# A fused chunk-select attention and ELU MLP on one core: the first batch prepared by four heads, and a step of the ELU moved to another engine

## The chip, the cores and the metric

The kernel runs on one core of one Trainium2 chip. The metric is device time in microseconds, the median of three runs. A core has five engines that work at the same time, each through its own list of instructions in order: PE (TensorE, matrix products), DVE (VectorE), ACT (ScalarE), POOL (GpSimd) and SP (SyncE, which here only issues DMAs).

## The reference

Four batches of eight heads, 768 positions, head dimension 64. For each head the keys are cut into 24 chunks of 32. A query's bound for a chunk is the sum over the 64 dimensions of the larger of q times the chunk's minimum and q times its maximum; the six causal chunks with the largest bounds are kept, and softmax attention runs over the kept, causal keys. The result, 3072 rows of 512, goes through an MLP with ELU in between.

```python
k_min, k_max = np.min(k_chunks, axis=3), np.max(k_chunks, axis=3)
ub = np.sum(np.maximum(q[..., None, :] * k_min, q[..., None, :] * k_max), axis=-1)   # shapes shortened
ub = np.where(causal, ub, -1e9)
top_chunks = np.argsort(ub, axis=-1)[..., -6:]
scores = np.where(sel & (pos[:, None] >= pos[None, :]), scale * q @ k.T, -1e9)
attn = softmax(scores) @ v
h = x @ w_in                                    # x: 3072 x 512, w_in: 512 x 2048
g = np.where(h > 0.0, h, np.exp(np.minimum(h, 0.0)) - 1.0)
out = g @ w_out                                 # 2048 x 512
```

The larger of the two products is computed as q * min + relu(q) * (max - min): one product of the turned queries with the chunk minima, one of their positive parts with the differences.

## The kernel before, in words

Heads go in pairs `u` (16 of them; four to a batch), and two pairs make a quad `g`. Each pair's 768 queries go in two halves `hf` of 384. Scores are computed transposed, keys on partitions and queries along the row, so that the exponentials (ACT, L675) can be used as weights of the products with V (`psO`, L707) without a turn. The selection is added to the scores by the product itself: the score product has 88 rows, 64 of the head dimension and 24 of a one-hot pattern `econ` in `lhs` against a 0/1 row per chunk in `rhs`, times -40000. The output of a pair is normalised (`on`, L720 and L723), turned by PE (`psT`, L732) and copied into `xT` (L735). When all four pairs of a batch have their `xT` for a half, the MLP's first products for it can start.

**The MLP** (`mlp`). For each half of a batch 16 blocks `fc` of 128 hidden units: four products into a bank `psH` (L757), exp on ACT into `e` (L767), and then one of three ways to finish the ELU. In blocks listed in `BOTH`, ACT makes relu in place (L772) and DVE makes min(e - 1, relu) (L775). In the last batch (`FAST`) DVE makes min(e, 1) - 1 and a maximum with h. In all others DVE makes t = max(e - 1, h) (L796) and then min(max(h, 0), t) (L801). The results `gT` go through the second products (`psM`, L814), ACT copies the sums out (L822) and SP stores them. The MLP of a batch runs beside the attention of the next.

**The first batch** (`first_prep`). Nothing can be hidden there. K and Q come in 256-byte rows, 128 positions on the partitions, each half of a pair in a DMA per head (L464; Q of the first two pairs from ACT's queue). PE turns them with an identity (L483, 48 products in float32); ACT copies K into `lhs` (L488) and Q into `qt` (L506), and makes the positive part `qa` (L510); DVE takes minima and maxima per chunk from PSUM (L493) and their difference (L500); POOL casts Q into `rhs` (L526) and V into `vext` (L517). The later batches (`pair_prep`) load in 128-byte pieces, turn on DVE (L403, L421), reduce there (L407) and cast on POOL.

**The selection** (`quad_sel`), for a quad and half: 16 products on tiles of 64 rows and 32 columns (L556), a turn of 32x32 blocks by DVE (L573), the eight largest per query and block (L585), a comparison with the sixth (L590), the turn back into `selt` (L596), and POOL copies of it into `rhs` (L607). The first batch's causal mask is one more product per diagonal block, an identity with `trineg` (L654); later ones are masked by POOL after the exponential (L694).

**The order** is made ahead of time by `Plan`: every operation has an engine, a duration, a priority, what it reads and writes and which buffers it takes; `order` simulates the engines with these durations and always takes what can start first, by priority among those ready. The order on each engine is then fixed in the program. Buffers are limited by `caps`; eight PSUM banks are shared as two double banks `S2` (scores) and four single ones (`ps`, with limits for `psH`, `psO`, `psT`, `psM` and `psMT`). `WHEN` names the operations that must be done before POOL asks for each piece of the MLP's weights.

## Time and profile before

| | |
|---|---|
| median of three runs | 284.86 us (284.71 to 284.96) |
| profiled execution | 283.3 us from the first to the last instruction, 1.56 us under the median |
| PE busy | 263.8 us, 93% |
| DVE busy | 207.3 us, 73% |
| ACT busy | 198.4 us, 70% |
| POOL busy | 125.2 us, 44% |
| granted TensorE clock | 0.976 on average |
| read from HBM, written | 27.26 MB, 6.29 MB |

The profile is one execution, recorded by the hardware. A line such as L757 is a line of the kernel before. Engines overlap, so shares do not add up. "Busy" of PE counts each product from its start to its modelled end, and products are pipelined: the time that a product really costs is the distance from its start to the next start. The same holds, less strongly, for DVE.

### The profile page before, as it was taken

To read this page: it belongs to the slowest core of one execution; us is meant where nothing else is said; L and a number is where in the kernel's file an instruction comes from. 1 tells how busy PE (TensorE), PEld (TensorE's weight loads), DVE (VectorE), ACT (ScalarE), POOL (GpSimd) and SP (SyncE) were. 2 spreads that over 40 slices of the span, in tenths; PEclk is the share of its full clock that TensorE was granted. 3 is DMA by queue.
4 is the path that set the end of the run, shared out by engine and by line. 5 is a ranking of instruction groups with operands and counts; after the bars stand their busy time and mean duration, and the time that the engine had idled before them with its cause. 6 is when DMAs were issued, how large, how long until landed. Compare 5 with 4: busy or idle time off the path is not lost.

```text
span 283.3 us, 7007 instructions
## 1 busy us (share of the span) xinstructions
PE 263.8 (93%) x2584; PEld 160.2 (57%) x2584; DVE 207.3 (73%) x563; ACT 198.4 (70%) x373; POOL 125.2 (44%) x235
## 2 busy tenths in 40 slices
PE   2887599999989999889999999999999999999994
PEld 2676357665546656465655566656565656555541
DVE  8827676798999998899989467967685424767610
ACT  4969379876498569999969967885856764545311
POOL 6547842046399689789558361611132201000000
PEclk9959779999999999999999999999999999999999
DMA  9878999988769899999984010001101101000111
GB/s 169 185 172 176 209 203 198 184 143 158 166 131 170 132 138 195 176 158 138 145 157 94 37 39 2 37 2 39 38 2 38 39 37 39 37 0 37 39 74 74
DMA packets 120993, 29.81 MB, mean 105 GB/s; under 512 B 113792, under 2 KB 117888, under 8 KB 120960
## 3 DMA queue, kind: packets, MB, share of 16 engines
q1 hardware_dynamic: 115136, 24.78, 46.4%
q0 software_dynamic: 4224, 4.19, 9.4%
q10 hardware_dynamic: 1600, 0.39, 0.7%
q8 instruction: 20, 0.33, 0.5%
q14 instruction: 13, 0.11, 0.1%
HBM read 27.26 MB, written 6.29 MB: 118 GB/s over the span
## 4 chain that ended last, share of the span: by engine, by line
PE 70%; ACT 10%; DVE 8%; DMA 5%; issue 3%; POOL 2%; SPq 1%; DVEq 0%; POOLq 0%; ACTq 0%
PE psM L814 18%; PE psH L757 16%; PE psS L648 9%; PE psS L757 7%; PE psMT L814 7%; PE psO L707 6%; ACT pt L675 5%; DMA stage<-in_k_dram 3%; PE psS L556 3%; DMA gT<-in_k_dram 1%; ACT e L767 1%; DVE gT L775 1%; DVE thr L585 1%; PE psT L732 1%; ACT lhs L488 1%
## 5 line engine op out<-in xcount | busy, mean ns | idle before, releaser
L675 ACT ACTIVATE pt<-psS 128x768 bf16<-128x768 f32 (+1 forms) x120 | 90.4, 798 | 6.5 <-PE psS L648 3.8
L757 PE MATMUL psH<-xT,w_in_sb 128*128 128x384 bf16 x384 | 75.9, 330 | 0.0
L814 PE MATMUL psM<-w_out_sb,gT 128*128 128x512 bf16 x288 | 72.2, 379 | 0.4 <-ACT xT L735 0.3
L757 PEld LDWEIGHTS <-w_in_sb 128*128 128x128 bf16 x512 | 48.2, 98 | 34.9 <-issue 2.6
L767 ACT ACTIVATE e<-psH 128x384 f32<-128x384 f32 x96 | 47.7, 518 | 25.2 <-PE psH L757 22.8
L648 PE MATMUL psS<-rhs,lhs 88*128 88x384 bf16 (+4 forms) x304 | 55.1, 292 | 4.2 <-ACT pt L675 1.9
L814 PEld LDWEIGHTS <-gT 128*128 128x128 bf16 x384 | 35.7, 97 | 35.0 <-issue 0.7
L694 POOL TENSOR_SCALAR_AFFINE_SELECT pt<-pt 128x256 bf16<-128x256 bf16 (+1 forms) x48 | 25.1, 527 | 45.5 <-ACT pt L675 42.5
L796 DVE SCALAR_TENSOR_TENSOR t<-e,psH 128x384 bf16<-128x384 f32 x56 | 30.1, 544 | 16.7 <-ACT e L767 16.3
L648 PEld LDWEIGHTS <-lhs 88*128 88x128 bf16 x304 | 29.1, 101 | 17.4 <-issue 5.4
L607 POOL COPY rhs<-selt 24x192 bf16<-24x192 bf16 (+1 forms) x64 | 27.0, 422 | 25.3 <-DVE selt L596 21.4
L526 POOL CAST rhs<-qt 64x768 bf16<-64x768 f32 (+1 forms) x40 | 28.3, 707 | 15.5 <-ACT qt L506 7.7
L707 PEld LDWEIGHTS <-pt 128*128 128x128 bf16 x672 | 28.0, 98 | 11.3 <-issue 3.2
L707 PE MATMUL psO<-vext,pt 128*128 128x65 bf16 x672 | 31.8, 195 | 1.8 <-DVE gT L801 0.8
L801 DVE SCALAR_TENSOR_TENSOR gT<-psH,t 128x384 bf16<-128x384 f32 x56 | 30.4, 547 | 1.1
L775 DVE SCALAR_TENSOR_TENSOR gT<-e,psH 128x384 bf16<-128x384 f32 x40 | 21.3, 536 | 10.9 <-ACT psH L772 8.9
L526 POOL CAST lhs<-kt 64x768 bf16<-64x768 f32 x24 | 19.7, 821 | 19.4 <-DVE kt L403 15.1
L767 ACT ACTIVATE e<-psS 128x768 f32<-128x768 f32 x16 | 13.0, 811 | 18.9 <-PE psS L757 18.9
L757 PE MATMUL psS<-xT,w_in_sb 128*128 128x384 bf16 x128 | 23.2, 326 | 0.0
L814 PE MATMUL psMT<-w_out_sb,gT 128*128 128x512 bf16 x96 | 22.5, 379 | 0.0
L735 ACT ACTIVATE xT<-psT 128x384 bf16<-128x384 bf16 x32 | 16.2, 506 | 8.2 <-PE psT L732 8.2
L772 ACT ACTIVATE psH<-psH 128x384 f32<-128x384 f32 x40 | 20.6, 521 | 0.0
(57 smaller groups left out, 287.4 us busy)
## 6 DMA issues: line engine op xcount, KB each, us to landing
out_dram<-osb SPq DMA_DIRECT2D x24, 256.0 KB, 2.0
stage<-in_k_dram SPq DMA_DIRECT2D x48, 96.0 KB, 4.1
stage<-in_q_dram SPq DMA_DIRECT2D x48, 96.0 KB, 3.6
vd<-in_v_dram SPq DMA_DIRECT2D x24, 192.0 KB, 3.8
w_in_sb<-in_moe_w_in_dram POOLq DMA_DIRECT2D x4, 512.0 KB, 9.4
w_out_sb<-in_moe_w_out_dram POOLq DMA_DIRECT2D x4, 512.0 KB, 9.0
gT<-in_k_dram SPq DMA_DIRECT2D x16, 96.0 KB, 3.0
gT<-in_v_dram SPq DMA_DIRECT2D x16, 96.0 KB, 2.5
```

The lines of the kernel that those rows point to most:

```text
L526: nc.gpsimd.tensor_copy(out=o, in_=i)
L607: eng.tensor_copy(out=dst.rearrange("c h (i two x) -> c h i two x", two=2, x=32)[:, :, :, odd, :], in_=tiles[st][r0:r0 + NCH, c0:c0 + n].r ...
L648: nc.tensor.matmul(p_s[:, hd, pc:pc + w], lhsT=tiles[pt_["kb"]][0:64 + NCH, hd, 128 * kb:128 * kb + 128], rhs=tiles[pt_["qb"]][0:64 + NCH, ...
L675: lambda bs=bs, pt=pt, wtot=wtot, lo=lo, at=at: nc.scalar.activation(out=tiles[pt][:, :, lo:lo + wtot], in_=tiles[bs[0]][:, :, at:at + wto ...
L694: nc.gpsimd.affine_select(out=a, in_=a, compare_op=AOT.is_ge, fill=0.0, base=0, pattern=pat, channel_multiplier=-1)
L707: nc.tensor.matmul(po[:, hd, qi, :], lhsT=tiles[pt][:, hd, off:off + 128], rhs=tiles[pt_["vx"]][:, 6 * hd + kb, :], start=(kb == 0), stop= ...
L757: nc.tensor.matmul(ph, lhsT=w_in_sb[:, kk, f0:f0 + 128], rhs=tiles[XT[4 * b + kk]][:, c0:c0 + HALF], start=(kk == 0), stop=(kk == NKK - 1))
L767: lambda e=e, view=view: nc.scalar.activation(out=tiles[e][:, 0:step], in_=view(), func=AF.Exp),
L775: lambda e=e, view=view, fc=fc, gt=gt: nc.vector.scalar_tensor_tensor(out=tiles[gt][:, fc:fc + step, :], in0=tiles[e][:, 0:step], scalar=1 ...
L796: lambda e=e, t=t, view=view: nc.vector.scalar_tensor_tensor(out=tiles[t][:, 0:step], in0=tiles[e][:, 0:step], scalar=1.0, in1=view(), op0 ...
L801: lambda t=t, view=view, fc=fc, gt=gt: nc.vector.scalar_tensor_tensor(out=tiles[gt][:, fc:fc + step, :], in0=view(), scalar=0.0, in1=tiles ...
L814: nc.tensor.matmul(pm, lhsT=tiles[gt][:, fc, 128 * tt:128 * tt + 128], rhs=w_out_sb[:, fc, :], start=(fc == 0), stop=(fc == NFC - 1))
```

## The change

It touches the first batch, the ELU and the planner.

- **Loads of the first batch** (`first_load`): K and Q come by head, 32 partitions of 6 pieces of 512 bytes (two neighbouring positions), so that four heads of a quad stand on the four groups of 32 partitions; V comes by 128 positions of four heads. The first half's Q is issued from ACT's queue.
- **Turning** (`first_prep`): DVE turns 32x32 blocks of a whole quad at once, 768 elements a partition, with the output regrouped; minima and maxima are taken from that; ACT casts K, POOL casts Q. PE's float32 turns, ACT's copies of K and Q and the difference on DVE go; the difference and its spreading into a block-diagonal `kmd` are on POOL.
- **Bounds** (`first_sel`): four products of 128 rows and 128 columns with `kmd`, for a whole quad and half.
- **Scores** (`first_scores`): each head's scores in two products of 32 rows (dimensions 0 to 31 and 32 to 63) and one of 24 rows that adds the selection, straight from `selt`; the four heads of a quad stand on four row groups. The causal mask is a product of 32 rows and 32 columns per quarter of a diagonal block and head (`below`, `corner`). A piece takes both double banks.
- **`lhs` and `rhs`** get their selection rows and zeros after the first batch, by DMA from `econ` and by POOL.
- **The ELU**: in the first three batches t = min(e, 1) - 1 is made by POOL (`HELP`), and DVE makes max(t, h). `BOTH` has 8, 8 and 4 blocks a half where it had 4, 12 and 4.
- **The planner**: it models the TensorE clock by windows, has a list of corrections to priorities (`RANK`), issues loads by readiness, and the weights wait for other operations. `caps` has two `psO` and two `psT`, and three `km`.

```diff
-BOTH = {0: (1, 5, 9, 13), 1: (0, 1, 2, 3, 4, 5, 8, 9, 10, 11, 12, 13), 2: (1, 5, 9, 13), 3: ()}
-def WHEN(q_in, left, out):
-    return (left(3, 0), out(0, 0), out(1, 0), out(2, 0), left(1, 1), left(1, 1), left(3, 1), left(3, 1))
+BOTH = {0: (1, 3, 5, 7, 9, 11, 13, 15), 1: (1, 3, 5, 7, 9, 11, 13, 15), 2: (1, 5, 9, 13), 3: ()}
+HELP = {0: range(16), 1: range(16), 2: range(16), 3: ()}
+RANK = {
+    80: 17.15, 158: 0.88, 160: 0.85, 178: 0.83, 180: 1.06, 182: 0.96, 184: 0.96, 186: 0.96, 188: 0.97,
...
+        o.prio = prio + RANK.get(o.n, 0.0)
...
+                    rank = o.ready if e == "DMA" and o.raw > -15 else o.prio
...
-            o.end = r + o.dur
+            o.end = r + (self.clocked(r, o.dur, act) if o.eng == "PE" else o.dur)
...
-    caps = {"S2": 2, "ps": 4, "H": 3, "O": 1, "T": 1, "M": 2, "MT": 2,
+    caps = {"S2": 2, "ps": 4, "H": 3, "O": 2, "T": 2, "M": 2, "MT": 2,
...
+    def rows(kb):
+        for hd in range(2):
+            nc.sync.dma_start(out=kb[64:96, hd, :], in_=econ[64:96])
...
+        def load(i, src, h, eng):
+            def f():
+                o0 = 768 * (2 * g + i)
+                eng.dma_start(
+                    out=tiles[sg].rearrange("p a b -> p (a b)")[32 * h:32 * h + 32, o0:o0 + 768].rearrange("c (m x) -> c m x", m=6),
+                    in_=src[4 * g + h, 6 * hf:6 * hf + 6].rearrange("m c x -> c m x"))
...
+        def turn(i, t):
             def f():
+                o0 = 768 * (2 * g + i)
+                nc.vector.transpose(
+                    out=tiles[t].rearrange("p (e m c j) -> p m j e c", e=2, c=32, j=2),
+                    in_=tiles[sg].rearrange("p a b -> p (a b)")[:, o0:o0 + 768].rearrange(
+                        "p (m j e i) -> p m j e i", m=6, j=2, e=2))
...
+        def ub():
+            pu = ps(bu, [P, HALF], F32)
+            for w in range(2):
+                for e in range(2):
+                    src = tiles[qd["qa", hf] if w else qd["qt", hf]].rearrange("p (e t) -> p e t", e=2)
+                    nc.tensor.matmul(pu[:, 0:n], lhsT=tiles[kmd[g]].rearrange("p (w e x) -> p w e x", w=2, e=2)[:, w, e],
+                                     rhs=src[:, e, lo:HALF], start=(w + e == 0), stop=(w + e == 2))
...
+            def sc(segs=segs, bs=bs, chosen=chosen):
+                for (b_, c0, w, pc) in segs:
+                    for e in range(3 if chosen else 2):
+                        for h in range(4):
+                            r = slice(32 * h, 32 * h + (NCH if e == 2 else 32))
+                            lhsT = (econ if e == 2 else tiles[kb][:, e])[r, 128 * b_:128 * b_ + 128]
+                            rhs = tiles[st][r, c0 - SEL0:c0 - SEL0 + w] if e == 2 else tiles[qb][r, e, c0:c0 + w]
+                            nc.tensor.matmul(tiles[bs[h // 2]][:, h % 2, pc:pc + w], lhsT=lhsT, rhs=rhs,
+                                             start=(e == 0), stop=(e == (2 if chosen else 1) and c0 >= 128 * b_ + 128))
+                    x1 = min(4, (c0 + w - 128 * b_) // 32)
+                    for x in range(max(0, (c0 - 128 * b_) // 32), x1):
+                        o0 = pc + 128 * b_ + 32 * x - c0
+                        for h in range(4):
+                            r = slice(32 * h, 32 * h + 32)
+                            nc.tensor.matmul(tiles[bs[h // 2]][:, h % 2, o0:o0 + 32], lhsT=below[r, x], rhs=corner[r],
+                                             start=False, stop=x == x1 - 1)
...
-                fast = FAST[b]
+                help_ = fc in HELP[b]
+                fast = FAST[b] or help_
                 if fast:
-                    add("DVE", 0.32 + 0.00021 * step * HALF, pr,
-                        lambda e=e, t=t: nc.vector.tensor_scalar(
+                    add("POOL" if help_ else "DVE", 0.15 + 0.00090 * step * HALF if help_ else 0.32 + 0.00021 * step * HALF, pr,
+                        lambda e=e, t=t, eng=nc.gpsimd if help_ else nc.vector: eng.tensor_scalar(
                             out=tiles[t][:, 0:step], in0=tiles[e][:, 0:step], scalar1=1.0, scalar2=1.0,
                             op0=AOT.min, op1=AOT.subtract),
```

378 lines of the change are left out of this document (236 added, 142 removed), and 8 rows, old and new, of tables (RANK, caps).

## The prediction

> **What bounds the kernel now.** I read the page's first line, then the busy time of each engine in stretches, cut where the trace changes character, first of all at the first product of the MLP (L757, 34.59 us). Columns: stretch, its length, busy time of PE, PEld, DVE, ACT, POOL with instruction counts, granted TensorE clock, DMA share, GB/s.
>
> ```profile
> span 283.3 us, 7007 instructions
> 0.00:34.59 34.59, 22.88 (x309) 18.58 (x309) 23.43 (x90) 23.06 (x53) 22.44 (x57) 0.86 0.94 181
> 34.59:60.00 25.41, 25.38 (x256) 16.76 (x249) 19.09 (x50) 22.04 (x41) 7.29 (x13) 0.93 1.24 192
> 60.00:100.00 40.00, 39.01 (x426) 22.16 (x425) 38.83 (x114) 27.45 (x51) 28.32 (x49) 1.00 0.85 145
> 100.00:160.00 60.00, 57.38 (x612) 34.88 (x611) 54.31 (x139) 53.61 (x106) 45.86 (x78) 1.00 0.88 145
> 160.00:262.00 102.00, 101.89 (x913) 59.74 (x912) 66.00 (x166) 67.21 (x117) 21.31 (x41) 1.00 0.07 28
> 34.59:38.40 3.81, 3.81 (x21) 1.83 (x14) 3.19 (x18) 1.38 (x3) 2.94 (x5) 0.51 1.42 213
> ```
>
> From 34.59 us on PE is the bound: it is idle 0.03 us up to 60, 1.0 up to 100, 2.6 up to 160 and 0.1 up to 262. Before 34.59 nothing is full; that is the pipe that fills. The last row shows that the first 3.8 us after it run at half clock. So the time is: when the first L757 starts (t1), plus PE's work from there, plus clock lost there, plus PE's few idle moments and the tail. The change can act on each of the first four, and work that PE does ahead of t1 counts only where it delays t1.
>
> What ends the filling is in the timeline (start, length, instruction, releaser in brackets):
>
> ```profile
> 32.69 0.50 PE L732 MATMUL psT<-ident_b,on 128*128 128x128 bf16 x3 [2.95 <-DVE on L723]
> 33.23 0.49 ACT L735 ACTIVATE xT<-psT 128x384 bf16<-128x384 bf16 x1 [2.87 <-PE psT L732]
> 34.59 2.74 PE L757 MATMUL psH<-xT,w_in_sb 128*128 128x384 bf16 x8
> ```
>
> PE waits 2.95 us for DVE's `on` of the fourth pair. From the end of that wait to a possible first product are 32.69, 33.23, 33.72: about 1.1 us.
>
> **Term A, t1.** Removed ahead of t1: 48 PE transposes, ACT's copies of K and Q, and ten DVE copies of `econ`. Added on DVE: eight turns of 128x768. Loads become 36 on SP and 8 on ACT's queue, each 96 KB of 512-byte rows (V 128 KB), where 44 on SP and 4 on ACT stood. First what SP pays for one load, and its landing:
>
> ```profile
> 0.81 3.46 SPq L464 DMA_DIRECT2D gT<-in_k_dram  x6
> 12.08 1.02 SPq L464 DMA_DIRECT2D gT<-in_k_dram  x2
> 13.14 1.02 SPq L464 DMA_DIRECT2D gT<-in_q_dram  x2
> gT<-in_k_dram SPq DMA_DIRECT2D x16, 96.0 KB, 3.0
> ```
>
> Two loads start 1.06 us after the two before them: 0.53 us each, which I keep for the new shapes, since no row here shows that fewer rows are issued faster. The four K of quad 0 start at 0.81 to 2.4 and land at 5.4. DVE's constants take under 4.5 us after 0.9 and are done about then. From there the order of the changed kernel puts on DVE, up to the fourth `on`: nine 128x768 turns, ten reductions, 30 of the MAX8, the bounds' turns, comparisons and turns back, four reciprocals and four `on`. Their cost is start to start in a stretch where DVE runs without a gap:
>
> ```profile
> 145.34 0.58 DVE L573 STREAM_TRANSPOSE ubt<-psS 128x384 f32<-128x384 f32 x1
> 145.98 0.54 DVE L801 SCALAR_TENSOR_TENSOR gT<-psH,t 128x384 bf16<-128x384 f32 x1
> 146.90 1.04 DVE L585 MAX8 thr<-ubt 128x8 f32<-128x14 f32 x12
> 147.87 0.17 DVE L720 RECIPROCAL rc<-psO 128x6 f32<-128x6 f32 x1
> 147.96 0.93 DVE L421 STREAM_TRANSPOSE qt<-stage 128x768 f32<-128x768 f32 x1
> 148.82 0.51 DVE L723 TENSOR_TENSOR on<-psO,rc 128x384 bf16<-128x384 f32 x1
> 149.26 0.53 DVE L796 SCALAR_TENSOR_TENSOR t<-e,psH 128x384 bf16<-128x384 f32 x1
> 153.36 0.95 DVE L407 TENSOR_REDUCE km<-kt 128x24 f32<-128x768 f32 x1
> 154.23 0.54 DVE L775 SCALAR_TENSOR_TENSOR gT<-e,psH 128x384 bf16<-128x384 f32 x1
> 156.09 0.45 DVE L590 TENSOR_TENSOR selv<-ubt,thr 128x288 bf16<-128x288 f32 x1
> 156.45 0.55 DVE L775 SCALAR_TENSOR_TENSOR gT<-e,psH 128x384 bf16<-128x384 f32 x1
> 156.92 0.57 DVE L596 STREAM_TRANSPOSE selt<-selv 128x384 bf16<-128x384 bf16 x1
> 157.41 0.51 DVE L775 SCALAR_TENSOR_TENSOR gT<-e,psH 128x384 bf16<-128x384 f32 x1
> ```
>
> A turn is 0.86, a reduction 0.87, one MAX8 0.97/12 = 0.081, reciprocal and `on` 0.09 + 0.44; the bounds' turn 0.64, the comparison 0.36 and the turn back 0.49 for 384 columns, half of it for 192. So 9 x 0.86 = 7.7; 10 x 0.87 = 8.7; 30 x 0.081 = 2.4; 4 x 0.53 = 2.1; bounds' turns 3 x 0.64 = 1.9 (two full, two halves), comparisons 2 x 0.36 = 0.7, turns back 2 x 0.49 = 1.0: 24.5 us. DVE waits, too. The last K of quad 1's second half is SP's 32nd load: it starts at 0.81 + 31 x 0.53 = 17.2 and lands at 20.2, while DVE, at its own pace, asks for it at about 17.5. The same for quad 0 costs about 0.3 earlier, which shortens the second wait: 2.7 together. `on` ends at 5.4 + 24.5 + 2.7 = 32.6, and with 1.1 + 0.1 for the transposes and the copy t1 = 33.8: **-0.8 us**. The small edits of this stage (memsets and `corner` on POOL, casts of whole quads, the first weights asked for earlier) lie beside this DVE chain. Bounds: no wait for loads gives 31.1; the first weights' 1 MB in the way of the last K and Q, at the 181 GB/s of this stretch, up to 5.5 us: 39.
>
> One link in it grows: the bounds' products. Before, 16 products on 64x32 tiles:
>
> ```profile
> 70.29 0.40 PE L556 MATMUL psS<-qt,km 64*32 64x96 f32 x16
> 70.48 0.37 PE L556 MATMUL psS<-qa,km 64*32 64x96 f32 x16
> 70.78 1.04 PE L814 MATMUL psM<-w_out_sb,gT 128*128 128x512 bf16 x4
> 71.75 0.56 PE L556 MATMUL psS<-qt,km 64*32 64x192 f32 x16
> 72.10 0.53 PE L556 MATMUL psS<-qa,km 64*32 64x192 f32 x16
> 72.56 1.47 PE L757 MATMUL psH<-xT,w_in_sb 128*128 128x384 bf16 x8
> ```
>
> 96 columns take 0.49 us, 192 take 0.81: 0.32 for 96 columns more, and 0.17 fixed. Sixteen products over eight tiles are two deep, so a column costs 0.32/192 = 1.67 ns. Four products of 384 columns, one after another, are then 2.56 us where 0.81 stood. PE has room for that ahead of t1, as long as the clock is full; at half clock two of them add 5 us to PE and about 2.5 to DVE's chain.
>
> **Term B, clock after t1.** Today 3.81 us at 0.51 of the clock lose 1.9 us, after PE's 2.95 us of idling. In the changed order two pieces of quad 0's second-half scores and two pairs' P·V stand ahead of the first L757 in that place, so I take the clock as granted: **-1.9**; the other end is 0.
>
> **Term C, scores left after t1.** Prices: 384 columns, and a short product with its own weights:
>
> ```profile
> 68.41 1.95 PE psH L757 x12
> 239.05 0.70 PE psO L707 x22
> ```
>
> 0.1625 us for 384 columns, 32 ns for a 65-column pair. Left today: four pairs x 2 heads x 1920 columns = 40 x 0.1625 = 6.5, and 24 mask products of 128 columns (a third of 0.1625) = 1.3: 7.8. Left afterwards: 2 quads x 3 products x 1920 columns, four heads at a time on 32-row tiles: 30 x 0.1625 = 4.9, less the two pieces ahead of t1 (1.0); 96 mask products of 32 columns; and the 0.17 fixed per tiled block for 8 pieces, 1.4. A 32-column product lies between 12 ns (16 tiled records start in 0.19 us above) and 32 ns; I take 22, halfway: 2.1. Sum 7.4: **-0.4**. Bounds: at 12 ns and without the fixed part -2.8; with no two tiles at once 4 x 3.9 + 3.1 + 1.4 = 20.1, +12.3. The Trainium skill (TensorE: Matmul & The Clock Gate, section "Wait — 56ns, not 53.3ns?") says that starts of products never come closer than about 25 ns, however short; by it the 96 take 2.4 us and C is -0.1. The 12 ns above stand against it, unless two records are one product.
>
> **Term D, the ELU.** All 56 t move from DVE to POOL, leaving one DVE step per block; two batches' counts of blocks that take ACT's second pass change by +8 and -8.
>
> ```profile
> L796 DVE SCALAR_TENSOR_TENSOR t<-e,psH 128x384 bf16<-128x384 f32 x56 | 30.1, 544 | 16.7 <-ACT e L767 16.3
> L517 POOL CAST vext<-gT 128x384 bf16<-128x384 f32 x8 | 3.9, 507 | 0.3
> L772 ACT ACTIVATE psH<-psH 128x384 f32<-128x384 f32 x40 | 20.6, 521 | 0.0
> 116.54 0.49 PE L648 MATMUL psS<-rhs,lhs 88*128 88x384 bf16 x2 [1.25 <-ACT pt L675]
> 124.89 0.54 PE L707 MATMUL psO<-vext,pt 128*128 128x65 bf16 x12 [0.83 <-DVE gT L801]
> ```
>
> DVE loses 30 us. POOL's t has the size of the cast in the second row; I take its 0.51, and as upper end twice the DVE row, 1.09. Batch 1's 16 t fall largely into 100 to 160: POOL 45.9 + 8.1 = 54 of 60 us, DVE 54.3 - 4.4 = 50, ACT 53.6 - 4.2 = 49: the fullest engine stays near 54. Batch 0's 16 t meet a POOL with room (35.6 of 65.4 us), batch 2's 24 one with more (21.3 of 102). Batch 0's eight extra passes cost ACT 4.2 us where it is busy 22.0 of 25.4; the copies it loses ahead of t1 do not help there, which speaks for some new PE waits. What can be won is PE's idle 3.6 us of 60 to 160, of which the last two rows show the largest: **-1.0**, between -3.6 and, with POOL full, the plus of the first rival. The new fills of `lhs` rows (ten DMAs, 5.3 us of SP) and `rhs` zeros go in once the loads are out; SP's cover is that batch 1's scores are far away: 0, and if that cover is gone 5.3 us at the start of batch 1.
>
> **The sum.** -0.8 - 1.9 - 0.4 - 1.0 = -4.1 on 283.3, so a span of 279.2. The median of the three runs is 284.86, 1.56 over the span of the profiled execution; with the same 1.56, **280.8 us**.
>
> **The rivals.** (1) *POOL becomes the bound of 100 to 160, slower.* For it: POOL is the fullest engine there even at 0.51; against it: the cast row. At 1.09 per t POOL has 45.9 + 17.4 = 63.3 us to do; busy 95% it needs 66.6, so +6.6 in place of -1.0: 288.4. It decides from a t of 0.9 us on: (64 x 0.95 - 45.9)/16, where the stretch grows by what the rest saves. The Trainium skill (GPSIMD Engine Reference, section 4.1, Engine selection) speaks for this: elementwise work belongs on VectorE, GpSimd being about twice as slow; but it limits that to two inputs and calls one input roughly line-rate, and t has one. Chance 0.14. (2) *The turns with regrouped rows cost DVE more.* No row shows them; `on` also writes regrouped and costs 0.44 for 384 columns, against it. At half as much again 8 x 0.43 = 3.4 us: 284.2; at twice 287.7. Chance 0.10. (3) *Late and cold*: the weights delay the last K, and the clock is halved around t1: A +2.5, B 0, so 286.0; milder, 284.5. For it: DMA at 0.94 in this stretch, and PE sparsely used ahead of t1. Chance 0.13. (4) *The tiles do not run side by side*, the change not doing what it says: 280.8 + 12.7 = 293.5 or more. The 64x32 tiles above overlap, against it. Chance 0.06. (5) *DVE's relief shows in full*: t1 32, D -3.6: 276.4. Chance 0.14.
>
> **How the numbers follow.** The forecast has 0.43, with a range of its own of 278 to 283.5 from halves of the bounds of A, C and D. 0.2% (0.57 us) is about what a measurement of this kernel tells from no change. Faster: 0.43 + 0.14 + 0.05 of rivals 2 and 3 in their mildest form = 0.62. Same: 0.08, from 2 and 3 at 284.2 to 285.4. Slower: the other 0.10 of these, and 1 and 4: 0.30. The range 275.5 to 288.5 leaves out the tiles' rival, the dear end of rival 2 and the far ends of 1 and 5, less than 0.2.
>
> **What would show it.** The first up product at 33 to 35 us at full clock (A, B); turns of 128x768 at 0.95 us and DVE without long gaps between 5 and 32 us (A); score pieces of 384 columns, without masks, in about 0.7 us (C); t on POOL near 0.5 us and POOL below 56 us busy between 100 and 160 (D). A t over 0.9 us, turns over 1.2 us, four tiles taking four times 0.16 us, or a first product after 37 us would make it wrong.

## The result: 11% slower, with POOL's step at three times its forecast price

| | before | after |
|---|---|---|
| median | 284.91 us (284.71 to 288.35, 4 runs) | 317.11 us (316.87 to 318.06, 4 runs) |
| profiled execution | span 283.3 us | span 316.3 us, 318.06 us in all |
| first up product (t1) | 34.59 us | 40.66 us |
| span from there | 248.7 us | 275.6 us |

The ratio is 1.109, 95% interval 1.100 to 1.118. Forecast were 280.8 us and a range of 275.5 to 288.5. (Some executions, of the kernel before and of several versions, run at a lower granted clock and take some per cent longer; ratios leave them out.) Both parts of the time went the wrong way: t1 came 6.1 us later than before, and what follows it took 26.9 us more.

The page of the changed kernel: span, busy time by engine, and the chain that ended last by engine and by line.

```profile
span 316.3 us, 7243 instructions
PE 265.6 (84%) x2736; PEld 154.2 (49%) x2736; DVE 186.4 (59%) x485; ACT 194.4 (61%) x349; POOL 200.9 (64%) x283
PE 38%; POOL 31%; DVE 8%; issue 8%; DMA 8%; ACT 4%; SPq 3%; POOLq 0%; DVEq 0%; ACTq 0%
POOL t L939 17%; PE psM L968 10%; PE psS L910 7%; PE psMT L968 7%; PE psH L910 5%; POOL rhs L763 5%; POOL pt L847 4%; DMA gT<-in_q_dram 3%; PE psO L860 3%; POOL rhs L683 2%; DMA gT<-in_k_dram 2%; DVE gT L944 2%; PE psS L806 2%; ACT pt L828 2%; POOL vext L487 1%
```

PE's work is nearly that of before (263.8 us), but PE alone is no longer the bound: `t`, the step that the change moved to POOL, is the largest line of the chain. Stretches cut much as in the prediction (columns as there):

```profile
24.00:40.00 16.00, 10.67 (x152) 6.95 (x150) 12.54 (x47) 7.42 (x13) 7.48 (x12) 0.89 1.14 169
60.00:100.00 40.00, 34.82 (x469) 19.81 (x467) 27.75 (x68) 28.55 (x53) 29.66 (x41) 1.00 0.76 134
100.00:160.00 60.00, 51.12 (x588) 29.66 (x579) 47.60 (x146) 42.06 (x80) 56.52 (x80) 1.00 0.80 133
160.00:260.00 100.00, 89.36 (x831) 52.17 (x829) 47.68 (x135) 68.78 (x126) 78.77 (x94) 1.00 0.10 30
```

Between 60 and 260 us PE is idle 5.2 + 8.9 + 10.6 us, where it had been idle 3.7 in all; POOL is the fullest engine from 100 to 160 (56.5 of 60). The groups of `t` and of the DVE step behind it (count, busy, mean ns, idle time before and its releasers), and the waits:

```profile
L939 POOL TENSOR_SCALAR t<-e 128x384 bf16<-128x384 f32 x56 | 83.3, 1494 | 21.4 <-ACT e L920 18.8 <-issue 1.8
L944 DVE TENSOR_TENSOR gT<-t,psH 128x384 bf16<-128x384 bf16 x56 | 30.9, 552 | 62.1 <-POOL t L939 61.5 <-PE psS L659 0.6
DVE gT L944 <- POOL t L939: 61.5, 48, 3.2
PE psH L910 <- DVE gT L944: 13.1, 18, 1.6
```

One `t` takes 1.49 us where 0.51 was assumed: 83 us of POOL for 56 of them. DVE waits for it 48 times, and PE, whose banks `psH` are freed by that DVE step, 18 times.

The first stretch, on DVE and then on PE (start, length, instruction, wait before it and its releaser):

```profile
6.34 0.97 DVE L548 STREAM_TRANSPOSE kt<-gT 128x768 f32<-128x768 f32 x1
18.56 0.98 DVE L548 STREAM_TRANSPOSE kt<-gT 128x768 f32<-128x768 f32 x1 [3.25 <-DMA gT<-in_q_dram]
26.49 0.98 DVE L548 STREAM_TRANSPOSE kt<-gT 128x768 f32<-128x768 f32 x1 [4.12 <-DMA gT<-in_k_dram]
DVE ubt L619 <- PE psMT L611: 0.9, 1, 0.9
40.66 0.49 PE L910 MATMUL psH<-xT,w_in_sb 128*128 128x384 bf16 x2
41.36 3.40 PE L910 MATMUL psH<-xT,w_in_sb 128*128 128x384 bf16 x10 [0.21 <-ACT xT L888]
```

DVE starts at 6.3, waits 3.3 and 4.1 us for the second half's K, and ten products at 41.36 take 3.40 us: clock is lost here again.

### The profile page after: what moved, and what is told of

Read it like the earlier page. It is cut to its first block, busy times and chain, and to the rows that moved or that the text cites. A ratio compares the mean times of both kernels' runs of the same rounds, so it can differ in the third digit from the quotient of the medians.

```text
span 316.3 us, 7243 instructions
## 1 busy us (share of the span) xinstructions
PE 265.6 (84%) x2736; PEld 154.2 (49%) x2736; DVE 186.4 (59%) x485; ACT 194.4 (61%) x349; POOL 200.9 (64%) x283
## 4 chain that ended last, share of the span: by engine, by line
PE 38%; POOL 31%; DVE 8%; issue 8%; DMA 8%; ACT 4%; SPq 3%; POOLq 0%; DVEq 0%; ACTq 0%
POOL t L939 17%; PE psM L968 10%; PE psS L910 7%; PE psMT L968 7%; PE psH L910 5%; POOL rhs L763 5%; POOL pt L847 4%; DMA gT<-in_q_dram 3%; PE psO L860 3%; POOL rhs L683 2%; DMA gT<-in_k_dram 2%; DVE gT L944 2%; PE psS L806 2%; ACT pt L828 2%; POOL vext L487 1%
## 5 line engine op out<-in xcount | busy, mean ns | idle before, releaser
L828 ACT ACTIVATE pt<-psS 128x768 bf16<-128x768 f32 (+3 forms) x120 | 88.3, 775 | 22.5 <-PE psS L806 12.2
L939 POOL TENSOR_SCALAR t<-e 128x384 bf16<-128x384 f32 x56 | 83.3, 1494 | 21.4 <-ACT e L920 18.8
L944 DVE TENSOR_TENSOR gT<-t,psH 128x384 bf16<-128x384 bf16 x56 | 30.9, 552 | 62.1 <-POOL t L939 61.5
L920 ACT ACTIVATE e<-psH 128x384 f32<-128x384 f32 x96 | 46.4, 499 | 27.4 <-PE psH L910 21.7
L968 PEld LDWEIGHTS <-gT 128*128 128x128 bf16 x384 | 36.1, 98 | 35.9 <-issue 1.1
L806 PE MATMUL psS<-rhs,lhs 88*128 88x384 bf16 (+2 forms) x216 | 38.0, 290 | 2.1 <-DMA out_dram<-osb 1.1
L683 POOL CAST rhs<-qt 64x768 bf16<-64x768 f32 (+1 forms) x28 | 23.2, 828 | 6.3 <-DVE qt L472 4.1
L806 PEld LDWEIGHTS <-lhs 88*128 88x128 bf16 x216 | 19.3, 97 | 12.6 <-issue 2.7
L763 POOL COPY rhs<-selt 24x192 bf16<-24x192 bf16 (+1 forms) x48 | 20.2, 421 | 5.7 <-DVE selt L753 3.5
L976 ACT ACTIVATE osb<-psM 128x512 f32<-128x512 f32 x18 | 10.8, 600 | 16.9 <-PE psM L968 16.9
L659 PE MATMUL psS<-rhs,lhs 32*128 32x384 bf16 (+4 forms) x176 | 9.7, 296 | 13.7 <-ACT lhs L561 9.5
```

Source lines behind the costliest of these rows:

```text
L683: nc.gpsimd.tensor_copy(out=o, in_=i)
L763: nc.gpsimd.tensor_copy(out=dst.rearrange("c h (i two x) -> c h i two x", two=2, x=32)[:, :, :, odd, :], in_=tiles[st][r0:r0 + NCH, c0:c0 ...
L806: nc.tensor.matmul(p_s[:, hd, pc:pc + w], lhsT=tiles[pt_["kb"]][0:64 + NCH, hd, 128 * kb:128 * kb + 128], rhs=tiles[pt_["qb"]][0:64 + NCH, ...
L828: lambda bs=bs, pt=pt, wtot=wtot, lo=lo, at=at: nc.scalar.activation(out=tiles[pt][:, :, lo:lo + wtot], in_=tiles[bs[0]][:, :, at:at + wto ...
L920: lambda e=e, view=view: nc.scalar.activation(out=tiles[e][:, 0:step], in_=view(), func=AF.Exp),
L939: lambda e=e, t=t, eng=nc.gpsimd if help_ else nc.vector: eng.tensor_scalar(out=tiles[t][:, 0:step], in0=tiles[e][:, 0:step], scalar1=1.0, ...
```

## Experiments

### What POOL's step costs

**t back on DVE.** The changed kernel with the ELU of before.

```diff
-BOTH = {0: (1, 3, 5, 7, 9, 11, 13, 15), 1: (1, 3, 5, 7, 9, 11, 13, 15), ...
-HELP = {0: range(16), 1: range(16), 2: range(16), 3: ()}
+BOTH = {0: (1, 5, 9, 13), 1: (0, 1, 2, 3, 4, 5, 8, 9, 10, 11, 12, 13), ...
+HELP = {0: (), 1: (), 2: (), 3: ()}
```

> The changed kernel with the ELU as before: no t on POOL, and the old lists of blocks that take ACT's second pass. Theory P (the price of t on POOL, 1.49 us where 0.51 was taken, carries what is lost after the first up product; the new first batch carries the rest): the first up product stays near 41 us as in the changed kernel, against 34.6 before, and what follows falls back to the 248.7 us of before, so 289 to 292 us. Rival S (the new first batch and its order disturb the later batches as well): over 300. Rival F (the new first batch is no loss by itself, the late t holds it up, too): first up product before 36 us, 280 to 285.

Measured: 289.62 us (287.24 to 290.03), in a later series of runs; span of the profile 285.5, t1 38.89. Going by the two medians, the ELU's part of the change is 27.5 of the 32.2 us. The other parts together still lose, by a late t1: what follows t1 takes 246.6 us, 2.1 less than in the kernel before.

**The ELU alone, in the kernel before.** `BOTH` and `HELP` of the change, POOL's `t` as there.

> The kernel before with the ELU part alone: t of the first three batches on POOL as one instruction of two steps, and the new lists of blocks with ACT's second pass. Theory P: the first up product stays at 34.6 us and the rest grows by about the 26 us by which it grew in the changed kernel, 305 to 314 us, with t at 1.49 us. Rival Q (t is dear only beside the new first batch's traffic): t near 0.5 us and 280 to 287 us.

Measured: 321.81 us (319.53 to 327.06), more than expected: what follows t1 grew by 39.3 us here, and by 26.9 in the changed kernel. Why it is dearer here was not followed. t1 is 33.48, so nothing of it comes from the start:

```profile
L787 POOL TENSOR_SCALAR t<-e 128x384 bf16<-128x384 f32 x56 | 83.4, 1493 | 21.0 <-ACT e L768 19.8
```

The price is the same in another surrounding, 1493 ns: it belongs to the operation, and not to the new first batch's traffic (rival Q).

**One step on POOL in place of two.** POOL makes only min(e, 1); DVE subtracts and takes the maximum in one instruction.

```diff
-  t = (e min 1.0) subtract 1.0      # POOL
-  gT = t max h                      # DVE, two inputs
+  e = e min 1.0                     # POOL, in place
+  gT = (e subtract 1.0) max h       # DVE, scalar_tensor_tensor
```

> The changed kernel with POOL's t cut to one step, min(e, 1) in place in float32; the subtraction goes into DVE's second step, which stays one instruction. If the price hangs on the second step (theory P2), the POOL instruction takes about 0.5 us like a cast of that size, and the time falls to 287 to 293 us, the first up product still near 41. If it hangs on scalar arithmetic on POOL as such (rival P1), it stays at 1.2 to 1.5 us and the time at 310 to 318.

Measured: 303.87 us (302.88 to 304.67), between the two cases. One step takes 1.17 us, far nearer to rival P1 than to the 0.5 of theory P2.

```profile
L939 POOL TENSOR_SCALAR e<-e 128x384 f32<-128x384 f32 x56 | 65.0, 1166 | 23.2 <-ACT e L920 22.4
```

**Prices by themselves.** A kernel with little but POOL instructions, six of each kind (`cp` cast, `min` and `sub` one step, `ms` min and subtract, `am` multiply and add), and min and subtract on DVE (`dv`); the outputs hold zeros.

> A kernel that leaves the computation out and only runs, six times each and one after another, POOL instructions on 128 partitions: a cast of 384 elements from float32 to bf16, one-step minimum and one-step subtraction of the same size, one-step minimum to float32, the two-step minimum and subtraction of 192, 384 and 768 elements, the same to float32 and from bf16, a two-step product and sum; and the two-step form on DVE. Theory P2: casts and one step about 0.5 us, every two-step form 1.4 to 1.5 us at 384, growing with the elements at 3.5 ns each or more. Rival P1: one step as dear as two. Rival M: min alone is dear and product and sum are not. DVE about 0.3 us.

```profile
L87 POOL CAST a_cp<-src 128x384 bf16<-128x384 f32 x6 | 3.2, 540 | 3.6 <-DMA src<-in_moe_w_out_dram 3.6
L91 POOL TENSOR_SCALAR a_sub<-src 128x384 bf16<-128x384 f32 x6 | 7.1, 1178 | 0.0
L95 POOL TENSOR_SCALAR a_ms<-src 128x384 bf16<-128x384 f32 x6 | 9.1, 1509 | 0.0
L99 POOL TENSOR_SCALAR a_ms<-src 128x768 bf16<-128x768 f32 x6 | 16.8, 2798 | 0.0
L105 POOL TENSOR_SCALAR a_am<-src 128x384 bf16<-128x384 f32 x6 | 3.3, 549 | 0.0
L107 DVE TENSOR_SCALAR a_dv<-src 128x384 bf16<-128x384 f32 x6 | 3.5, 586 | 0.2
```

Beside its size (2798 ns for 768 elements) the kind sets the price: one step with a scalar costs 2.2 casts, two steps 2.8, but the pair multiply and add costs one. Min and subtract take 0.59 us on DVE, so the move to POOL made that step 2.6 times as dear. Theories P2 and P1 fell; rival M was right on the pair, but subtract alone is as dear as min alone (1.18 and 1.24 us).

**The pair multiply and add in the kernel.** The same place in the same order; only the arithmetic of two instructions changes. For h above 0, max(h, 0) = h is the smaller, below it e^h - 1 is.

```diff
-  t = (e min 1.0) subtract 1.0      # POOL
-  gT = t max h                      # DVE
+  t = (e mult 1.0) add -1.0         # POOL
+  gT = (h max 0.0) min t            # DVE, scalar_tensor_tensor
```

> The changed kernel with one difference in the ELU's POOL step: it makes u = e times 1 plus (-1) in place of t = min(e, 1) minus 1, and DVE then makes min(max(h, 0), u) in one instruction of two inputs; every instruction stands in the same place of the same order. Theory P (POOL's price per operation is the cause behind t1; a product and a sum costs the cast's 0.55 us): POOL instructions of 0.52 to 0.58 us, busy POOL about 148 us, PE idle in 160 to 260 us back under 4 us, time 286 to 290 us, about that of the run with t on DVE (289.6), with the first up product still at 38.5 to 41 us. Rival O (the order that was planned with POOL in the ELU is bad whatever the price): over 295 us. Rival S (POOL and DVE take turns at a shared port, so that POOL's work delays DVE's): POOL instructions near 0.55 us but DVE's own instructions dearer, time 291 to 297 us.

Measured: 288.5 us (286.35 to 289.46), 0.8% over the kernel before on the same chip (ratio 1.008, 1.003 to 1.014).

```profile
L939 POOL TENSOR_SCALAR t<-e 128x384 bf16<-128x384 f32 x56 | 28.4, 511 | 34.4 <-ACT e L920 31.7 <-issue 2.0
100.00:160.00 60.00, 59.20 (x667) 36.01 (x666) 52.69 (x144) 51.82 (x96) 49.84 (x94) 1.00 0.80 135
160.00:260.00 100.00, 100.00 (x885) 59.33 (x883) 50.95 (x130) 67.90 (x122) 38.62 (x73) 1.00 0.09 32
```

511 ns, PE idle 0.8 us from 100 to 160 and not at all from 160 to 260; span 287.7, 28.6 less than with the dear step. Theory P held, with t1 at 41.73 a little past its 41; an order that is bad whatever the price (O) and turns at a shared port (S: DVE's step behind it still takes 548 ns) fell. The planner had made this order with 0.50 us for POOL's step (0.15 + 0.00090 x 384). What an order made for 1.49 us would have saved was not tried, so the 28.6 us are the price of the dear step in an order made for a cheap one.

**The same in the kernel before.**

> The kernel before, with the change's ELU alone (every t piece that was on DVE in the first three batches on POOL, the change's choice of pieces with the Relu on ACT), POOL making u = e times 1 plus (-1), DVE min(max(h, 0), u). The prediction's term D, which took 0.51 us for the POOL step, gives -1.0 us: 282 to 284 us against about 283.3 to 284.5 for the kernel before on the same chip. Theory P: that term was mis-sized in the price alone, so this gives 281.5 to 285 us. Rival O (more work on POOL's queue delays DMA issues, casts and counts whatever the price): 286 to 295 us.

Measured: 287.09 us (286.14 to 293.4), ratio 1.007 (1.002 to 1.013); t1 34.70, t 516 ns. The price is right, and still it loses: from t1 to the end 250.7 us, 2.0 more than before. Theory P's 281.5 to 285 was missed and rival O's range fits this kernel; what exactly the order loses was not followed.

**Which kinds are cheap.** Again little but POOL instructions, outputs zero (`mul`, `add` and `max` one step; `mm` multiply and min, `ma` min and add, `aa` multiply and add, `ms` multiply and subtract).

> Nothing but POOL instructions of 128x384 from float32 to bf16, six of each kind: scalar multiply alone, scalar add alone, scalar max alone, multiply and min, min and add, multiply and add, multiply and subtract, and an addition of two tensors. Theory F (multiply and add have a fast path, alone or together; one min, max or subtract takes the instruction off it): 0.5 to 0.6 us for multiply, add, multiply and add; 1.15 to 1.25 for max; 1.45 to 1.55 for each pair with min or subtract. Theory G (only the pair of multiply and add is fast): 1.15 to 1.25 for each single one, 1.5 for every other pair.

```profile
L83 POOL TENSOR_SCALAR a_mul<-src 128x384 bf16<-128x384 f32 x6 | 7.1, 1189 | 3.6 <-DMA src<-in_moe_w_out_dram 3.6
L85 POOL TENSOR_SCALAR a_add<-src 128x384 bf16<-128x384 f32 x6 | 7.0, 1173 | 0.0
L87 POOL TENSOR_SCALAR a_max<-src 128x384 bf16<-128x384 f32 x6 | 7.1, 1178 | 0.0
L89 POOL TENSOR_SCALAR a_mm<-src 128x384 bf16<-128x384 f32 x6 | 9.1, 1508 | 0.0
L91 POOL TENSOR_SCALAR a_ma<-src 128x384 bf16<-128x384 f32 x6 | 9.0, 1507 | 0.0
L93 POOL TENSOR_SCALAR a_aa<-src 128x384 bf16<-128x384 f32 x6 | 3.2, 528 | 0.0
L95 POOL TENSOR_SCALAR a_ms<-src 128x384 bf16<-128x384 f32 x6 | 9.1, 1519 | 0.0
```

Theory G: of these only multiply together with add (`aa`) is cheap, 0.53 us. Each alone costs 1.17 to 1.19, and every other pair tried 1.51 to 1.52.

### Why the first up product is late

All these runs have the cheap POOL step, except the one with t on DVE. Start of the last K turn, t1, span and what lies between, in us:

| run | last K turn | t1 | span | span - t1 |
|---|---|---|---|---|
| cheap step, loads as in the change | 26.31 | 41.73 | 287.7 | 246.0 |
| V moved | 23.41 | 38.85 | 284.8 | 246.0 |
| weights later | 23.69 | 37.52 | 284.1 | 246.6 |
| weights later, 8 of 12 V loads out | 19.55 | 32.94 | 279.7 | 246.8 |
| V moved and weights later | 24.44 | 39.27 | 288.2 | 248.9 |
| weights later, t on DVE | 24.03 | 37.26 | 287.7 | 250.4 |
| both selections first, weights later | 24.11 | 36.88 | 290.8 | 253.9 |
| next batch's turns later, weights later | 23.70 | 36.11 | 287.3 | 251.2 |
| loads in order of need, weights later | 23.69 | 36.82 | 294.8 | 258.0 |

Each row is one execution. With the loads as in the change and only the ELU differing, four profiles have t1 at 38.89, 39.28, 40.66 and 41.73, with a granted clock of 0.79 to 1.00 between 24 and 40 us. So a t1 that differs by 1 or 2 us between two rows decides nothing by itself.

**V moved.** The due time of the first half's six V loads is raised.

```diff
-  pl + 1.2 + 0.01 * m, vload(m)
+  pl + (2.1 if hf == 0 else 1.2) + 0.01 * m, vload(m)
```

> The product-sum version of the changed kernel with the eight first-half V loads... that is the six V loads of the first half moved behind all K and Q loads of both halves on SP's queue (one number, their due time); nothing else. Theory L (the first stretch is bounded by the bytes of the loads in their order: 4.7 MB at about 210 GB/s, with V ahead of the second half's K): the last second-half K turn starts 3 to 6 us sooner than in the run without it (there about 25.7 us), the first up product at 34 to 37 us, time 3 to 5 us less. Rival C (the chain of DVE and of POOL and the cold clock set the first product, not the loads): the K turn sooner, but the first product within 1 us of that run's, time within 1 us. Rival V (attention then waits for V): first product later, time 1 to 3 us more.

Measured: 287.71 us, ratio 1.004 (0.9995 to 1.009). The last K's loads still stood behind nine V loads on SP's queue, since the planner's corrections delay them; the turn came 2.9 us sooner all the same, and t1 with it. What moved was the first weight transfer, which POOL asks for in its own order: at 16.50 us with the loads as in the change, ahead of the last K's, and at 21.27 here, behind them. First with the loads as in the change, then in this run: when POOL asks for the first weights, and the last three K loads (the last figure is their median time from issue to landing):

```profile
16.50 0.96 POOL L412 DMA_DIRECT2D w_in_sb<-in_moe_w_in_dram  x1
gT<-in_k_dram SPq DMA_DIRECT2D x3, 96.0 KB, 7.7
21.27 0.96 POOL L412 DMA_DIRECT2D w_in_sb<-in_moe_w_in_dram  x1
gT<-in_k_dram SPq DMA_DIRECT2D x3, 96.0 KB, 4.4
```

So this run speaks for the weights, and not for V.

**Weights later.** The first two transfers wait for the second half's Q of quad 1.

```diff
-  enumerate(((SELT[0], 0), (SELT[1], 0), out(0, 0), ...
+  enumerate(((QUAD[1]['qb'], 1), (QUAD[1]['qb'], 1), out(0, 0), ...
```

> The product-sum version of the changed kernel with the first two weight transfers (w_in, 512 KB each) asked only when the second half's Q of the second four heads has been cast, in place of when the first selections are done (about 17.5 and 31 us); nothing else. Theory W (the weight transfer at 17.5 us takes the loads' bandwidth): the last second-half K turn starts 2 to 2.5 us sooner than the about 25.7 us of the version without it, the first up product 1 to 2 us sooner unless it then waits for the weights, which land 7 to 9 us after about 31 us, 38 to 40 us. Theory L (bytes in their order, V ahead): the turn 2 us sooner at most and the time within 1 us. Rival: the first product waits for the weights and comes at 40 us or later, time 1 us more.

Measured: 285.81 us, ratio 0.998 (0.994 to 1.002): the level of the kernel before. Turn 2.6 and t1 4.2 us sooner, more than expected. The last three K loads land 4.9 us after their issue in place of 7.7, so theory W has the cause of the earlier turn. Of t1's 4.2 us a part may be clock: the granted clock of 24 to 40 us was 0.89 here and 0.79 without it. With t on DVE the same move (the run with t on DVE below) brought t1 forward by 1.6 us only, 38.89 to 37.26.

**Bytes taken away.** As the last, with two of three V loads of the first batch not issued.

```diff
-  vload(m)
+  (lambda: None) if m else vload(m)
```

> The product-sum version with the later weights, with eight of the first batch's twelve V loads not issued (two of every three; the V casts read the remaining third three times over, so the first batch's attention is of other values): 1.05 of 4.7 MB less, every other instruction in the same order. Theory L (the bytes ahead of the second half's K on the DMA engines set the turns of K and so the first up product): the turns of the second half's K at 15.5 to 16.5 and 21 to 22 us in place of 18.4 and 23.7, first up product at 34.5 to 36 us in place of 37.5, time 2 to 3 us less than 285.8. Theory Q (it is DVE's queue: the second four heads' K turn of the second half stands ahead of the first half's selection of those heads and holds it): the same shift for the turn, and the product sooner by what the selection is held less, 1 to 2 us. Rival C (what follows is the bound): product within 0.5 us of 37.5.

Measured: 281.55 us, ratio 0.990 (0.986 to 0.994).

```profile
15.81 0.98 DVE L548 STREAM_TRANSPOSE kt<-gT 128x768 f32<-128x768 f32 x1 [0.33 <-DMA gT<-in_q_dram]
19.55 0.94 DVE L548 STREAM_TRANSPOSE kt<-gT 128x768 f32<-128x768 f32 x1
32.94 3.29 PE L910 MATMUL psH<-xT,w_in_sb 128*128 128x384 bf16 x12
```

DVE's K turns wait for no load any more beyond 0.3 us, t1 is 32.94 (the forecast's bound without waits for loads was 31.1, its value 33.8), and the time 281.55, 0.7 over the forecast. Theory L, that what stands ahead of K sets t1, held even beyond its 34.5 to 36. But bytes are not told apart from issues here: six V loads fewer ahead of the last K also free SP of six issues of about 0.5 us. It was asked for at 15.3 us in place of 18.6, and landed 3.6 us after in place of 5.0, so 3.3 of the 4.7 us stand on SP's side. POOL's casts of V wait less, too. It is no version to use, since it leaves loads out.

**Both moves together**, on another chip.

```diff
-  enumerate(((QUAD[1]['qb'], 1), (QUAD[1]['qb'], 1), out(0, 0), ...
+  enumerate(((QUAD[0]['qb'], 1), (QUAD[1]['qb'], 1), out(0, 0), ...   # and V as above
```

> The product-sum version with both moves: the first-half V loads behind the K and Q loads of both halves, and the first two weight transfers asked when the second half's Q of the first and of the second four heads has been cast. Theory L (in the first stretch the bytes ahead of the second half's K and Q set the first up product, and after it TensorE is full): the last second-half K turn at 21 to 23.5 us (23.4 with V moved alone, 23.7 with the weights moved alone), the first up product at 35 to 37 us, and the time lower by as much as that product is earlier: 282 to 284 us, against 288.5, 287.7 and 285.8 us of the versions with neither, V, and weights moved. Rival C (what follows the last K turn, DVE's 24 us of work, POOL's casts and the bounds' products at a halved clock, is the bound by now): turn earlier, product still at 37 to 38.5 us, time within 1 us of 285.8. Rival V: attention and POOL's casts wait for V, product at 38 us or later, 286 us or more.

Measured: 290.25 us, ratio 1.013 (1.004 to 1.021). A miss: the two did not add, the turn came at 24.44, and twelve products at 39.27 took 3.60 us at a lower clock. They could hardly add: with V moved alone the weights were behind the last K already, and the gates here ask for the first weights at 23.0 us, where the later weights alone had 29.5.

**t on DVE, weights later**, run beside the one before: `BOTH` and `HELP` as in the first experiment, the gates as in the run with the weights later.

> The changed kernel with the ELU of the kernel before (t on DVE, the pieces with the Relu on ACT as before) and the first two weight transfers asked only when the second half's Q of the second four heads has been cast. It stands to the product-sum version with the same weights (285.8 us) as the ELU alone, at POOL's lower price, does. Theory D0 (TensorE is full after the first up product either way, so the ELU's placement is worth under 1 us here): 285 to 287 us with the first product at 36.5 to 38.5 us. Rival D1 (the prediction's term D at its own price, -1.0 us for t on POOL): 286.5 to 288 us with the same first product. Rival D2 (t on POOL costs, as it did in the kernel before, by 0.7%): 283 to 285 us.

Measured: 289.46 us, ratio 1.012 (1.006 to 1.019). t1 as expected, but 250.4 us behind it, 3.8 more than with t on POOL, on another chip; the time is above all three theories. Against that, t on DVE with the early weights had 246.6, and t on POOL 246.0. What the placement is worth seems to depend on the order made with it, more than term D allowed for; with different chips and single profiles this is not shown.

**DVE's order.** K's turn of quad 1 (and, in the second run, that of quad 0) behind the first half's selection of the same quad.

```diff
-  turn(0, kt), reads=[(sg, g, 0, h) for h in range(4)]
+  turn(0, kt), reads=[(sg, g, 0, h) for h in range(4)] + ([(SELT[1], 0)] if hf and g else [])
```

> The product-sum version with the later weights, and on DVE's queue the second half's K turn of the second four heads placed behind the first half's selection of those heads (bounds' turn, MAX8, comparison, turn back) in place of ahead of it; no load, no byte and no weight is moved. Theory Q: the selection no longer stands behind a turn that waits for its load; the bounds' turn of the second four heads, at 24.6 us before, starts at about 22.3, so the scores of the second four heads, AV, xT and the first up product come 2 to 3 us sooner: 34.5 to 36 us in place of 37.5, time 282.5 to 284 us against 285.8. Theory L (bytes): the last K turn lands as before and the second half follows as late, product within 1 us of 37.5, time within 1 us of 285.8.

> As the version with the later weights and the selection of the second four heads first, with also the first four heads' selection (the turn back to one row per head) ahead of their second half's K turn, which there waits 3.1 us for its load. Theory Q: a further 0 to 1.5 us off the first up product (34 to 35.5 us), 281.5 to 283.5 us, the fastest of these, if the scores of the first four heads that it frees were on the path; the price is a second half that comes later. Rival: the second half becomes the bound (its bounds and scores are late after the first up products, TensorE waits between 36 and 60 us by 1 us or more), 284 to 286 us.

Measured: ratios 1.053 (1.046 to 1.060) and 1.021 (1.014 to 1.028). In the second, t1 came only 0.6 us sooner than with the weights later alone, and then this (DVE twice, PE):

```profile
42.63 0.98 DVE L454 STREAM_TRANSPOSE kt<-stage 128x768 f32<-128x768 f32 x1 [4.63 <-DMA stage<-in_k_dram]
45.38 1.01 DVE L944 SCALAR_TENSOR_TENSOR gT<-psH,t 128x384 bf16<-128x384 f32 x2
45.98 1.44 PE L910 MATMUL psH<-xT,w_in_sb 128*128 128x384 bf16 x4 [5.31 <-DVE gT L944]
```

The new order put a K turn of the next batch, whose load lay behind the weights, ahead of the first step of the ELU, and PE stood 5.3 us. Theory Q gave a product 2 to 3 us sooner already by the first of the two moves: it did not come, and the order lost more than it won.

**The next batch's turns later, and loads in order of need.** First only K's turns of the next batch's first two pairs behind `xT`; then also SP's queue in order of need, with V of the second half last.

```diff
-  turn of the next batch's kt: reads=[kd]
+  reads=[kd] + ([(XT[3], u - 4)] if u in (4, 5) else [])
-  pl + 1.2 + 0.01 * m, vload(m)                         # second run only
+  (pl + 1.2 if hf else -6.30) + 0.01 * m, vload(m)      # and no RANK for the last K and Q
```

> The product-sum version with the later weights, and of the above only the second edit: the K turns of the next batch's first two pairs behind xT of the first batch's fourth pair. It takes 2.7 us of turn and reductions from DVE's queue ahead of the last normalisation before the first up product. Theory K (DVE's queue is full between 24 and 37 us, so what stands ahead counts): product at 34.5 to 36 us in place of 37.5, time 283 to 285 us against 285.8. Theory L (the loads set it): product at 37 us or later, time within 1 us.

> The product-sum version with the later weights and SP's queue in plain order of need: K of the first half, K and Q of the second half for the first four heads, V of the first half, K and Q of the second half for the second four, V of the second half last (in the version with V moved the planner's corrections still left nine V loads ahead of the last K); and the K turns of the next batch's first two pairs placed behind xT of the first batch's fourth pair, first and second half, so that no turn that waits for a late load stands ahead of the first blocks of the ELU. Theory L (bytes ahead of the second half's K): that K's turns by 16.5 and 22 us, first up product at 34 to 36.5 us, time 282 to 284.5 us, if nothing later stalls. Rival (the weights and the next batch's loads meet after 30 us: TensorE waits by 3 us or more between 38 and 60 us for gT, K or V): product as early, time 286 us or more.

Measured: 289.38 us, ratio 1.018 (1.014 to 1.021), and 297.34, ratio 1.044 (1.040 to 1.048). t1 36.1 and 36.8, just past what K and L gave, and it was lost again: PE waits 2.5 us in one place for POOL's copy of the selection in the first, and in the second POOL waits 4.9 us for the next batch's V with `t` queued behind it. With the loads in order the last K turn is at 23.69 as before, but it no longer waits for its load: the last K was asked for at 15.8 us and landed near 20.2, some 3.4 us sooner than with the weights later alone, and DVE did the selection and two normalisations first. t1 was then held elsewhere. The V of the second half is the last of the loads, POOL's casts of it wait for it, and the spreading of the second half's K into `osb` (the tile of `kmd`) stands behind them on POOL, with PE's bounds behind that, at a clock of 0.50:

```profile
23.99 0.96 POOL L589 CAST vext<-gT 128x384 bf16<-128x384 f32 x2 [5.02 <-DMA gT<-in_v_dram]
28.48 2.93 PE L613 MATMUL psMT<-qt,osb 128*128 128x384 f32 x4 [4.05 <-POOL osb L571]
```

So the order of the same bytes did bring K forward, and t1 did not follow, because each engine takes its list in order.

Two more runs lost as well: the planner told a landing of 4.0 us, ratio 1.015 (1.007 to 1.024), where 283.5 to 285 us or no change had been expected, and quad 1's selection first with the early weights, 1.029 (1.021 to 1.037), where 283.5 to 285.5 or, by bytes alone, 287 or more had been. No version tried that does the whole work beats the kernel before; the later weights reach it.

## Why the prediction was wrong, by its own steps

- **Term D is the step that failed.** The row that it was nearest to by size, the cast's 0.51 us, was of another kind. `t` took 1.49, above even the upper end of 1.09, which came from another engine. With the kind that does cost 0.51, in the same order, the span fell from 316.3 to 287.7: 28.6 us. The -1.0 itself is not settled: behind t1, t on POOL at 0.51 gave -0.6 us against t on DVE with the early weights, -3.8 with the later ones (both across chips), +2.0 in the kernel before.
- **Rival 1 is what happened**, with its mechanism (POOL full from 100 to 160, 56.5 of 60 us) and past its point of decision (0.9 us), but at 1.09 it had 288.4. With the measured 1.49 its own formula gives (45.9 + 16 x 1.49) / 0.95 = 73.4 for that stretch, 13.4 us more, half of what was lost. It looked at one stretch; the stalls are spread over 60 to 260, since `t` holds DVE (48 waits, 61.5 us) and with it a bank also where POOL is not full (78.8 of 100 us from 160 to 260, PE idle 10.6). The Trainium skill (GPSIMD Engine Reference, section 4.1, Engine selection) calls one input roughly line-rate; the runs bear that out for a cast (0.54 us) and for multiply with add (0.53), which is near the 0.59 of min and subtract on DVE, and not for min, max, subtract, or multiply or add alone (1.17 to 1.24).
- **Term A was mis-sized: t1 40.66 in place of 33.8, +6.9.** DVE's turns began at 6.34 in place of 5.4: +0.9. Waits for loads were 3.25 + 4.12 = 7.4 in place of 2.7: +4.7. SP asked for the last K at 18.6 us in place of 17.2; a load landed 3.9 us after its issue in the median, not 3.0, and the last three K, behind the first weights, 7.7 after. DVE waited 0.9 for the bounds' products, which the sum had at nothing. DVE's own chain took 25.7 in place of 24.5, +1.2, and the last step 0.3 in place of 1.2, -0.9, because the first two products did not wait for the fourth pair's `xT`. The bound "weights in the way" gave 39 and names what happened: without the weights in the way the turn of the last K came 2.6 us sooner and t1 1.6 to 4.2, without most V loads t1 another 4.6. Rival 3 (late and cold) happened too, with A +6.9 where it took +2.5.
- **Term B failed with it**: ten products at 41.36 took 3.40 us, where the prediction's 0.1625 for each make 1.6. With the weights later the clock was full there (nine in 1.62 us), with V bytes out it was not (twelve in 3.29).
- **Terms B, C and D behind t1, at the price taken**: 279.2 - 33.8 = 245.4 us forecast, 246.0 measured with the cheap step. So the sum from t1 on was off by 0.6. That is the sum alone, from one profile: of its terms only the lower price of the mask products and the lost clock were seen singly, and the -1.0 of D, as said, was not.
- **Right on the smaller points.** Turns with regrouped rows 0.97 us (rival 2 fell). Four tiles side by side (rival 4 fell):

```profile
47.22 0.50 PE L659 MATMUL psS<-rhs,lhs 32*128 32x384 bf16 x8
47.56 0.33 PE L659 MATMUL psS<-selt,econ 24*128 24x384 bf16 x4
47.72 0.26 PE L666 MATMUL psS<-corner,below 32*128 32x32 bf16 x16
47.91 0.34 PE L910 MATMUL psH<-xT,w_in_sb 128*128 128x384 bf16 x1
```

Twelve products of 384 columns start from 47.22 to 47.72, 0.50 us (0.7 was said). Sixteen mask products, as many as the program issues for four heads and four quarters, follow in 0.19 us: 12 ns each, the lower end of term C, and each record is one product. The 25 ns that the Trainium skill gives as the least distance of starts (TensorE: Matmul & The Clock Gate, section "Wait — 56ns, not 53.3ns?") do not hold here, between products on different tiles of the array.

## What to carry to other kernels

Price an operation that moves to another engine by a row of the same kind on that engine; if the trace has none, the upper end must not come from a different engine, and a chance of 0.14 was too small for an unmeasured kind. Rewrite the arithmetic into the cheap kind before giving the engine up: here the same function, as a product with a sum, took a third of the time, which won back 28.6 us, though nothing over the kernel before. At the start of a kernel count the bytes ahead of the last load that the chain needs, weights included, and not the issues alone; and look at what else each engine has in its list ahead of that chain, since a load that comes sooner helps only as far as the next wait. Compare such starts by several executions: t1 alone moved by 2.8 us between profiles with the same loads.

## What was not expected of the hardware

POOL's instruction with two scalars is cheap for one pair only of the five tried: multiply and add 0.53 us at 128x384, against 1.17 for an add alone, so that a multiplication put ahead of the add makes it 0.64 us cheaper. And longer rows did not make the loads a small matter: the changed kernel, with 512-byte rows, moved 196 GB/s in its first 24 us at a DMA share of 1.11, the kernel before 176 at 0.84. At 196 GB/s the first batch's 4.7 MB take 24 us, an estimate without the weights; the last K's turn started at 26.5. First the changed kernel, then the one before (columns as above):

```profile
0.00:24.00 24.00, 9.30 (x159) 7.86 (x160) 15.52 (x33) 8.56 (x18) 14.51 (x45) 0.93 1.11 196
```

```profile
0.00:24.00 24.00, 16.22 (x187) 13.98 (x188) 16.52 (x62) 16.31 (x38) 13.41 (x40) 0.86 0.84 176
```
